# Moving the plain stores and loads of a fused convolution and dense-layer gradient kernel from SyncE's queue to GpSimd's

## The chip, the cores and the metric

The kernel runs on one core of a Trainium2 chip. The metric is the device time of one execution in microseconds (us), of which the median over several runs is given. A profile is one execution of the same program recorded by the hardware profiler.

The core has five instruction queues that matter here. PE is TensorE (matmuls; PEld its weight loads), DVE is VectorE, ACT is ScalarE, POOL is GpSimd, and SP is SyncE, which does no arithmetic and only issues DMAs (its rows in the timeline are called SPq). Each queue is worked off strictly in the order in which its instructions were written: an instruction that waits for a semaphore holds up all that stand behind it on the same queue.

## The reference, cut to what matters

The network has four layers over a sequence of 2048 rows of width 448: gated long convolution (A), dense layer with SiLU (B), A again with the same weights, B again with the same weights. The kernel returns the output and the gradients for q, k, v, shift_k, ssm_k, ssm_D, w1 and w2.

```
def A(q, k, v, shift_k, ssm_k, ssm_D):
    k_shift = 4-tap causal filter of k with shift_k
    kv = k_shift * v
    y = irfft(rfft(kv, 4096) * rfft(ssm_k, 4096))[:2048] + kv * ssm_D
    return q * y
def B(x, w1, w2):
    return silu(x @ w1) @ w2          # 448 -> 1792 -> 448
x = A_q
x = x + A(layernorm(x), k, v, ...)
x = x + B(layernorm(x), w1, w2)
x = x + A(layernorm(x), k, v, ...)
x = x + B(layernorm(x), w1, w2)
out = x;  gradients by jax.vjp with grad_out
```

The convolution result y doesn't depend on x, so it is computed once and used by both A layers.

## The kernel before, in words

**Three stages.** The head (class Head) computes the spectra of ssm_k and kv by a two-stage transform built of matmuls, multiplies them, and transforms back to y (tile Ysb). It ends at about 95 us. The main part (class Flow) walks over 16 tiles of 128 rows. The end (class Tail) forms the two weight gradients and the gradients of k, v and ssm_k.

**One tile of the main part** goes through: norm, gate, norm (n1); up through w1 (ps_h), SiLU and its slope on ACT (aT, dT); down through w2 (ps_o); norm, gate, norm (n3); up, SiLU and down again; then the backward pass: grad_out up through the transposed w2 (ps_g), times the slope (ghT), down through the transposed w1 (ps_n), the backward norm and gate, and the same once more for the first layer. Several tiles are in flight at a time. Each norm takes the power -0.5 of the variance on POOL (rstd, line 651); DVE needs it for the normalized tile n (line 652).

**Transposes.** An up step needs its input transposed (tile nT). For most tiles this is done by two DMA transposes that SP issues (lines 665 and 666 for n and G, lines 827 and 828 for grad_out). Ten of them at the two ends of the main part are done on PE.

**What is kept for the end.** The weight gradients need aT (both layers) and ghT (both layers) of all 16 tiles, so these are written to DRAM, 448 KB each, 64 stores in all. ghT is stored as it is in runs of 256 bytes (GH0 and GH1, `store`, line 740). aT is first transposed by a DMA transpose to the tile `turned` (line 746, ring of two buffers) and then stored in rows of 3584 bytes (A0 and A1, line 747). Both kinds are issued by SP. The normalized rows (N_d), the two outputs and the loads of grad_out and A_q rows go through POOL.

**The end.** `jobs("w2")` and `jobs("w1")` each walk over seven pairs p of 256 rows of the weight gradient. For each pair and each of two groups gi (the two layers) `bring` loads a 1 MB block jb from DRAM, and PE runs 2 x 16 matmuls of 448 columns over it (line 1200). jb is a ring of three buffers; two blocks of w1 use the buffer of Minv instead. For w2 the block is a plain load (line 1144; SP, only those of the first two pairs POOL). For w1 it is a DMA transpose out of GH0 or GH1 (line 1142, SP). The moving operand of w1 is the reloaded n (nmov, line 1124, SP). Results of w2 are stored through POOL (line 1226), those of w1 through SP (line 1228). Between the matmuls of these jobs PE does the inverse transforms for the gradients of k, v and ssm_k.

**What sets the order.** No instruction order is written by hand. Every step is an `s.op` with a cost per engine that could do it, a priority and, for DMAs, a kind and a number of bytes. `Sched.plan` runs these through a list scheduler: an engine that is free takes the ready step of lowest priority, a DMA's end is planned from its bytes, a rate per kind (RATE) and a constant (TAIL). `Sched.emit` then writes every engine's instructions in the planned order. The table NUDGE shifts single priorities, keyed by tile and kind of step. So a changed cost, rate or nudge changes the order of all five queues, and the order stays as planned however late a transfer is at run time.

Of the kernel before, what the change touches and what calls it, by code (L numbers as in the profile page):

```python
# [21 lines left out]
P = 128  # L22
S = 2048
D = 448
F = 1792
# [108 lines left out]
class Sched:  # L134
# [4 lines left out]
    STEP = 20  # L139
    TAIL = 1.5  # L140
    EPS = 1e-9
    RATE = {"plain": 410e3, "turn": 400e3, "load": 400e3, "rows": 280e3, "line": 280e3, "swap": 240e3}

# [239 lines left out]
class Head:  # L383
# [11 lines left out]
    def run(self, pr):  # L395
# [23 lines left out]
        for b in range(4):  # L419
            self.load(lambda b=b: ksb[b][:], k.A_ssm_k[128 * b:min(128 * b + 128, D), :], [ksb[b]], pr, 524e3 if b < 3 else 262e3)  # L420
        m1f = lambda: M1[:].rearrange("p a c k -> p (a c k)")
# [6 lines left out]
        k.w2 = s.vb("res", "W2", [P, NF * D], BF16, "w2sb")  # L428
        self.load(lambda: k.w2[:].rearrange("p (c d) -> p c d", d=D), k.B_w2.rearrange("(c p) d -> p c d", p=P), [k.w2], pr + 0.5, 1605e3)
        k.w2T = [s.vb("E", "w2T", [P, 3 * F], BF16, "w2T"), s.vb("PM", "w2Tr", [P, F], BF16, "w2T")]  # L430
        s.op({"SP": 9}, lambda e: nc.sync.dma_start_transpose(out=k.w2T[0][:].rearrange("p (c f) -> p c f", f=F), in_=k.B_w2[:, 0:384]), w=k.w2T[:1], prio=pr + 0.6, dma=("turn", 1376e3))
        for j in range(3):
# [96 lines left out]
        def conv(h, jq, q):  # L529
            pc = self.unit([P, 4, 256], name="ps_cv")  # L530

            def cv(e):
                for u in range(4):
                    j = 4 * jq + u
                    for c in range(2):
                        for t in range(4):
                            js = (j - t) % J
                            o = 1 if j >= t else 0
                            nc.tensor.matmul(pc[:, u, c * DC:(c + 1) * DC], lhsT=kT[h]()[:, js // 4, c, js % 4, o:o + 128], rhs=diag[h]()[:, c, t, :], start=(t == 0), stop=(t == 3))

# [5 lines left out]
            s.op({"POOL": 0.6}, lambda e: nc.gpsimd.dma_start(out=_pm(k.KS_d[:])[:, 4 * jq:4 * jq + 4, ds], in_=ks[:]), r=[ks], w=[ksv], prio=q + 20, dma=("plain", 230e3))  # L546
            s.op({"DVE": 0.54}, lambda e: nc.vector.tensor_tensor(out=kvt[:], in0=ks[:], in1=V.t[:, 4 * jq:4 * jq + 4, ds], op=ALU.mult), r=[ks, vs[jq // 2]], w=[kvt], prio=q)
            for u in range(0, 4, 2):
                n2 = 4 * jq + u
                ps = self.unit([P, 2, 2, 256], name="ps_s1")  # L550

                def s1(e, u=u, n2=n2, ps=ps):
                    for w in range(2):
                        for c in range(2):
                            nc.tensor.matmul(ps[:, w, c, :D // 2], lhsT=M1[:, n2 + w, c, :], rhs=kvt[:, u + w, :], start=True, stop=True)

                s.op({"PE": 0.4}, s1, r=[kvt, m1s[n2 // 8]], w=[ps], prio=q + 0, hold=[A1v])
                for w in range(2):
                    s.op({"ACT": 0.47, "DVE": 0.54}, lambda e, w=w, n2=n2, ps=ps: _copy(nc, e, A1v[:, 56 * h:56 * h + 56, :, n2 + w, :].rearrange("p dh c ds -> p c dh ds"), ps[:, w, :, :D // 2].rearrange("p c (dh ds) -> p c dh ds", ds=4)),
                         r=[ps], w=avs[7 * h:7 * h + 7], prio=q + 0)  # L560
# [56 lines left out]
EARLY = 2  # L617
ROWS = (0, 128, 256, 320)
TURNED = ((0, 1), (1, 1), (3, 0), (3, 1), (4, 0), (14, 1), (15, 0))
NUDGE = {(1, "ch"): 4, (4, "ch"): 0.4, (5, "ch"): 0.6, (6, "ch"): 4, (7, "ch"): 7, (13, "ch"): -0.2, (4, "cv"): -3, (6, "cv"): 4.2, (7, "cv"): 7, (1, "gG"): -8, (12, "gG"): 4, (14, "gG"): 6, (1, "h1"): 52, (2, "h1"): -3, (8, "h1"): -14, (4, "h2"): 11, (1, "kt"): -5, (2, "kt"): -9, (3, "kt"): -22, (5, "n1"): 4, (12, "n1"): 6, (10, "n2"): 3, (13, "n2"): 7, (14, "n2"): 7, (6, "o1"): -1, (10, "o1"): -2, (0, "s1"): -8, (2, "s1"): -9, (5, "s1"): -1, (6, "s1"): 5, (7, "s1"): -3, (9, "s1"): 1, (14, "s1"): 0.4, (15, "s1"): 2, (8, "s2"): 8, (10, "s2"): -2, (13, "s2"): 16, (3, "t1"): -11, (1, "t3"): -11, (15, "t3"): 6, (14, "tG"): -12, (0, "tg"): -44, (0, "tk"): 3, (1, "tk"): 2, (2, "tk"): 1, (6, "tk"): 20, (7, "tk"): 3, (8, "tk"): 4, (9, "tk"): 5, (10, "tk"): 3, (11, "tk"): 2, (12, "tk"): 11, (13, "tk"): 4, (3, "tt"): -0.2, (1, "tv"): -8, (2, "tv"): 5, (3, "tv"): 2, (8, "tv"): 16, (11, "tv"): -4, (13, "tv"): -12, (0, "w1"): 59, (5, "w1"): 14, (6, "x1"): -20, (7, "x1"): -20, (8, "x1"): -6, (8, "x3"): -7, (12, "xG"): 56, (0, "y"): 31}  # L620
NT1 = {1: "nTG", 2: "nT3", 3: "nT3"}
# [5 lines left out]
class Flow:  # L627
# [32 lines left out]
    def turn(self, src, pr, tag, on_pe, after=()):  # L660
        nc, k, s = self.nc, self.k, self.s
        if not on_pe:
            nT = self.small(tag, (P, ND, P))
            nT.name = "nT"
            s.op({"SP": 1.65}, lambda e: nc.sync.dma_start_transpose(out=nT[:, 0:3, :], in_=src[:, 0:384]), r=[src], w=[nT], prio=pr - EARLY, dma=("turn", 98e3))
            self.last_rows = s.op({"SP": 1.2}, lambda e: nc.sync.dma_start_transpose(out=nT[:, 3, :], in_=src[:, 320:448]), r=[src], w=[nT], prio=pr - EARLY, dma=("turn", 33e3))
            return nT
# [65 lines left out]
    def store(self, src, nm, j, pr):  # L733
        nc, s, k = self.nc, self.s, self.k
        dst = k.rows_d[nm]
        if nm not in RAW:
            self.store_turned(src, nm, j, pr)
            return
        at = dst.rearrange("(a p) s -> p a s", p=P)[:, :, P * j:P * j + P]
        s.op({"SP": 0.45}, lambda e: nc.sync.dma_start(out=at, in_=src[:]), r=[src], w=[k.st_[(nm, j)]], prio=pr, dma=("rows", 458e3))  # L740

    def store_turned(self, src, nm, j, pr):
        nc, s, k = self.nc, self.s, self.k
        dst = k.rows_d[nm]
        an = self.small("turned", (P, NF, P))
        s.op({"SP": 1.6}, lambda e: nc.sync.dma_start_transpose(out=an[:], in_=src[:].rearrange("p a s -> p (a s)")), r=[src], w=[an], prio=pr, dma=("turn", 458e3))
        s.op({"SP": 0.4}, lambda e: nc.sync.dma_start(out=dst[:, j, :], in_=an[:].rearrange("p a f -> p (a f)")), r=[an], w=[k.st_[(nm, j)]], prio=pr + 3, dma=("plain", 458e3))

# [41 lines left out]
    def tile(self, j):  # L790
# [35 lines left out]
        gT.name = "nT"  # L826
        s.op({"SP": 1.55}, lambda e: nc.sync.dma_start_transpose(out=gT[:, 0:3, :], in_=g[:, 0:384]), r=[g], w=[gT], prio=at("tg", c - 4), dma=("turn", 98e3))
        s.op({"SP": 1.2}, lambda e: nc.sync.dma_start_transpose(out=gT[:, 3, :], in_=g[:, 320:448]), r=[g], w=[gT], prio=at("tg", c - 4), dma=("turn", 33e3))
        gh2 = self.grad_up(gT, s2, at("g", c + 11.3), [up2] if j else [], not j)
# [38 lines left out]
class Tail:  # L868
# [242 lines left out]
    def jobs(self, which, pr):  # L1111
# [6 lines left out]
        else:  # L1118
            nm = [s.vb("PF", ("A1", "B1v")[i], [P, NT, D], BF16, "nmov") for i in range(2)]
            nh = [[v.sub() for _ in range(2)] for v in nm]  # L1120
            for i in (1, 0):
                for h in range(2):
                    hs = slice(8 * h, 8 * h + 8)
                    s.op({"SP": 0.4}, lambda e, i=i, hs=hs: nc.sync.dma_start(out=nm[i][:, hs, :], in_=_pm(k.N_d[i][:])[:, hs, :]),
                         r=[k.st_[("n", i, j)] for j in range(8 * h, 8 * h + 8)], w=[nh[i][h]], after=self.done[i], prio=pr - 30 if i else pr + 0.5, dma=("plain", 917e3), behind=k.loads[-1 - i:][:1])
# [34 lines left out]
        for p in range(NF // 2):  # L1160
# [66 lines left out]
            else:  # L1227
                s.op({"SP": 0.4}, lambda e, o=o, p=p: nc.sync.dma_start(out=out7[:, :, 256 * p:256 * p + 256], in_=o[:].rearrange("p c u f -> p c (u f)")), r=[o], prio=q, dma=("plain", 230e3))

# [75 lines left out]
def _rest(k):  # L1305
# [43 lines left out]
    k.w1T = s.vb("PM", "w1T", [P, NF * D], BF16, "w1T")  # L1349
    s.op({"SP": 2.0}, lambda e: nc.sync.dma_start_transpose(out=k.w2T[1][:], in_=k.B_w2[:, 320:448]), w=k.w2T[1:], prio=-100, dma=("turn", 460e3))  # L1350
    for h in range(2):
# [51 lines left out]
```

## Time and profile before

| | us |
|---|---|
| three runs | 718.8, 716.04, 714.32 |
| median | 716.04 |
| profiled execution, its own time | 722.49 |
| profiled execution, span from first to last instruction | 720.7 |
| PE busy | 686.6 |
| DVE busy | 518.2 |
| ACT busy | 408.1 |
| POOL busy | 161.1 |

Mean granted TensorE clock over the span: 0.99. The head is the first 95 us or so, the main part lasts to about 475 us, the end takes the rest. A busy time is the union of an engine's instructions; PE's is from modelled ends of pipelined matmuls. DMA share is the mean busy share of the 16 DMA engines; in single stretches it can read a little over 1. In the waits view a row reads: who waited, for what, how much in total, how many times, the longest. In the timeline a row reads: start, length, engine, line, operation, tiles, how many merged, and in brackets the idle time before it and who ended it. SP's rows are issue times: how long the queue was held by the instruction.

### The profile page before, as it was taken

The page shows a single profiled execution, that of the slowest core. Times are in us where ns is not written, and L with a number is a line of the kernel's source. Part 1 is how long each engine was busy: PE and PEld are TensorE (multiplying, and loading weights), DVE is VectorE, ACT ScalarE, POOL GpSimd, SP SyncE. Part 2 cuts the span into 40 slices and gives each one's busy share as a digit, 9 for nine tenths or more (in the row PEclk, how much of TensorE's full clock was granted, in tenths as well). Part 3 has the DMA queues.
Part 4 walks back from the last instruction along what each step waited for, and adds up shares of the span by engine and source line. Part 5 has one row for each costly group of instructions (what it writes and reads, how often), then busy time and mean ns, then how long its engine had stood idle before and what let it go on. Part 6 is the DMA issues. An engine that isn't in the chain of part 4 may idle for free. (4 is left out here: it accounts for less than half of the span.)

```text
span 720.7 us, 18096 instructions
## 1 busy us (share of the span) xinstructions
PE 686.6 (95%) x7496; PEld 476.6 (66%) x7512; DVE 518.2 (72%) x1206; ACT 408.1 (57%) x497; POOL 161.1 (22%) x274
## 2 busy tenths in 40 slices
PE   6999898999999899999999999999999999799997
PEld 4887666677676676776767776655777755345553
DVE  4979888768988868898888976764699758960000
ACT  4889887676667456766567664324877540014111
POOL 1233253203232122223222123022133131100000
PEclk9999999999999899999999999999999999899999
DMA  9959999967797777797786979956799669997961
GB/s 324 274 145 267 396 190 204 203 161 182 172 201 163 157 162 161 164 184 190 181 172 147 190 202 286 249 150 196 236 377 325 193 223 305 259 230 167 199 143 27
DMA packets 269727, 150.50 MB, mean 209 GB/s; under 512 B 224302, under 2 KB 250334, under 8 KB 269260
## 3 DMA queue, kind: packets, MB, share of 16 engines
q1 hardware_dynamic: 254494, 102.39, 62.0%
q0 software_dynamic: 14384, 46.14, 20.9%
q8 instruction: 59, 0.97, 0.6%
q10 hardware_dynamic: 766, 0.80, 0.4%
q14 instruction: 24, 0.20, 0.1%
HBM read 50.68 MB, written 54.60 MB: 146 GB/s over the span
## 5 line engine op out<-in xcount | busy, mean ns | idle before, releaser
L1200 PEld LDWEIGHTS <-jb 128*128 128x128 bf16 x892 | 85.8, 98 | 83.2 <-DMA jb<-GH_d 5.6
L1200 PE MATMUL ps_d<-nmov,jb 128*128 128x448 bf16 x448 | 90.0, 358 | 5.1 <-DMA jb<-GH_d 5.1
L692 PE MATMUL ps_h<-nT,w1sb 128*128 128x128 bf16 x1344 | 88.1, 222 | 5.7 <-DMA nT<-n 4.4
L755 PE MATMUL ps_n<-w1T,ghT 128*128 128x448 bf16 x448 | 90.0, 352 | 0.0
L755 PE MATMUL ps_o<-w2sb,aT 128*128 128x448 bf16 x448 | 89.5, 352 | 0.0
L692 PE MATMUL ps_g<-nT,w2T 128*128 128x128 bf16 x1344 | 86.1, 219 | 2.3 <-DMA nT<-G 2.3
L692 PEld LDWEIGHTS <-w1sb 128*128 128x128 bf16 x1344 | 78.6, 99 | 11.0 <-issue 4.0
L692 PEld LDWEIGHTS <-w2T 128*128 128x128 bf16 x1344 | 77.8, 98 | 10.8 <-issue 2.7
L93 ACT CAST ghp<-ps_g 128x896 bf16<-128x896 f32 x62 | 56.2, 907 | 42.9 <-PE ps_g L701 33.1
L729 ACT ACTIVATE aT<-ps_h 128x896 bf16<-128x896 f32 x64 | 56.8, 916 | 26.1 <-PE ps_h L701 17.6
L651 POOL TENSOR_TENSOR rstd<-ve,mhalf 128x1 f32<-128x1 f32 x64 | 41.0, 641 | 122.0 <-DVE ve L648 121.9
L755 PEld LDWEIGHTS <-ghT 128*128 128x128 bf16 x448 | 43.1, 98 | 37.8
L755 PEld LDWEIGHTS <-aT 128*128 128x128 bf16 x448 | 42.9, 98 | 36.7
L779 DVE SCALAR_TENSOR_TENSOR junk<-u,n 128x448 bf16<-128x448 bf16 x64 | 39.9, 623 | 31.7 <-ACT u L858 30.7
L729 ACT ACTIVATE dT<-ps_h 128x896 bf16<-128x896 f32 x60 | 53.2, 916 | 15.4 <-PE ps_h L701 10.5
L858 ACT ACTIVATE u<-ps_n,rstd 128x448 bf16<-128x448 f32 x32 | 20.3, 634 | 54.0 <-PE ps_n L755 24.6
L729 ACT ACT_TABLE_LOAD x38 | 48.8, 1283 | 0.7
L95 DVE COPY do<-ps_dt 112x512 bf16<-112x512 bf16 x2 | 0.8, 425 | 62.5 <-PE ps_dt L1221 62.5
L93 ACT CAST dob<-ps_d 128x448 bf16<-128x448 f32 x14 | 7.4, 532 | 67.6 <-PE ps_d L1200 67.6
L1200 PE MATMUL ps_d<-G,jb 128*128 128x448 bf16 x224 | 45.5, 352 | 0.2
L1200 PE MATMUL ps_d<-gmov,jb 128*128 128x448 bf16 x220 | 45.4, 353 | 0.1
L646 DVE BATCH_NORM_STATS2 st<-x 128x6 f32<-128x448 bf16 x64 | 40.0, 626 | 1.6
(180 smaller groups left out, 1270.0 us busy)
## 6 DMA issues: line engine op xcount, KB each, us to landing
A_d<-turned SPq DMA_DIRECT2D x32, 448.0 KB, 3.4
GH_d<-ghT SPq DMA_DIRECT2D x32, 448.0 KB, 4.7
jb<-A_d SPq DMA_DIRECT2D x10, 1024.0 KB, 6.8
KK<-KK POOLq DMA_DIRECT2D x14, 256.0 KB, 5.1
spec_KV<-X POOLq DMA_DIRECT2D x7, 512.0 KB, 9.5
spec_K<-KK POOLq DMA_DIRECT2D x7, 512.0 KB, 9.6
N_d<-n POOLq DMA_DIRECT2D x32, 112.0 KB, 4.2
sp_c<-spec_KV POOLq DMA_DIRECT2D x14, 256.0 KB, 6.7
```

What stands on the lines that cost most here:

```text
L93: nc.scalar.copy(out, in_)
L95: eng.tensor_copy(out, in_)
L646: nc.vector.bn_stats(out=st[:], in_=x[:])
L651: s.op({"POOL": 1.0}, lambda e: nc.gpsimd.tensor_tensor(out=rs[:], in0=ve[:], in1=self.k.mhalf[:, 0:1], op=ALU.pow), r=[ve], w=[rs], prio=pr)
L692: nc.tensor.matmul(ps[:, i, :], lhsT=at(b, ft), rhs=nT[:, b, :], **f)
L729: prev = [s.op({"ACT": 0.93}, lambda e, i=i, fun=fun, out=out, late=late: nc.scalar.activation(out[:, 7 * i:7 * i + 7, :], c[:, 7 * i:7 * ...
L755: nc.tensor.matmul(po[:, :D], lhsT=a[:, ft, :], rhs=wt[:, ft * D:(ft + 1) * D], start=(ft == 0), stop=(ft == NF - 1))
L779: nc.vector.scalar_tensor_tensor(out=junk[:], in0=u[:], scalar=1.0, in1=n[:], op0=ALU.mult, op1=ALU.mult, accum_out=cp[:, 1:2])
L858: s.op({"ACT": 0.85}, lambda e: nc.scalar.activation(u[:], pn[:, :D], ACT.Identity, scale=r[:], accum_out=cp[:, 0:1]), r=[pn, r], w=[u, cp ...
L1200: nc.tensor.matmul(ps[:, :D], lhsT=rows(t, gi, u), rhs=at(t), start=(first and t == ts[0]), stop=(last and t == ts[-1]))
```

## The change

Four things are changed.

1. The 64 stores of aT and ghT (lines 740 and 747) are issued by POOL instead of SP, and so are the four loads of nmov (line 1124) and the seven stores of the w1 gradient (line 1228). The condition `first` in `bring` also becomes true for p of 5 and 6, so four more plain blocks of jb go through POOL. In the main part SP then issues transposes only.
2. The planner's numbers: SP's cost of the transposes (1.25 us for each nT; 4.5 instead of 9 for w2T, 1.5 instead of 2 for its rest), a cost of 0.6 us for each store that POOL issues, TAIL 1.6 instead of 1.5, a new rate "short" for the stores of the shifted k, and larger byte counts for the loads of ssm_k and w2 in the head.
3. The table NUDGE is another one, 83 entries with other keys and values.
4. No step is added, no arithmetic is changed, and no buffer count is changed.

```
-    TAIL = 1.5
+    TAIL = 1.6
-    RATE = {"plain": 410e3, ..., "swap": 240e3}
+    RATE = {"plain": 410e3, ..., "swap": 240e3, "short": 140e3}
...
-            self.load(... k.A_ssm_k ..., [ksb[b]], pr, 524e3 if b < 3 else 262e3)
+            self.load(... k.A_ssm_k ..., [ksb[b]], pr, (1020e3, 524e3, 820e3, 750e3)[b])
...
-        self.load(... k.B_w2 ..., [k.w2], pr + 0.5, 1605e3)
+        self.load(... k.B_w2 ..., [k.w2], pr + 0.5, 2350e3)
-        s.op({"SP": 9}, ... dma_start_transpose(out=k.w2T[0] ...
+        s.op({"SP": 4.5}, ... dma_start_transpose(out=k.w2T[0] ...
...
-            s.op({"POOL": 0.6}, ... out=_pm(k.KS_d[:]) ..., dma=("plain", 230e3))
+            s.op({"POOL": 0.6}, ... out=_pm(k.KS_d[:]) ..., dma=("short", 230e3))
...
-NUDGE = {(1, "ch"): 4, (4, "ch"): 0.4, (5, "ch"): 0.6, ...
+NUDGE = {(0, "ch"): -2, (1, "ch"): 1, (2, "ch"): -6, ...
...
-            s.op({"SP": 1.65}, ... dma_start_transpose(out=nT[:, 0:3, :] ...
-            self.last_rows = s.op({"SP": 1.2}, ... dma_start_transpose(out=nT[:, 3, :] ...
+            s.op({"SP": 1.25}, ... dma_start_transpose(out=nT[:, 0:3, :] ...
+            self.last_rows = s.op({"SP": 1.25}, ... dma_start_transpose(out=nT[:, 3, :] ...
...
-        s.op({"SP": 0.45}, lambda e: nc.sync.dma_start(out=at, in_=src[:]), ..., dma=("rows", 458e3))
+        s.op({"POOL": 0.6}, lambda e: nc.gpsimd.dma_start(out=at, in_=src[:]), ..., dma=("rows", 458e3))
...
-        s.op({"SP": 0.4}, lambda e: nc.sync.dma_start(out=dst[:, j, :], in_=an[:]...), ..., prio=pr + 3, dma=("plain", 458e3))
+        s.op({"POOL": 0.6}, lambda e: nc.gpsimd.dma_start(out=dst[:, j, :], in_=an[:]...), ..., prio=pr + 3, dma=("plain", 458e3))
...
-        s.op({"SP": 1.55}, ... dma_start_transpose(out=gT[:, 0:3, :] ...
-        s.op({"SP": 1.2}, ... dma_start_transpose(out=gT[:, 3, :] ...
+        s.op({"SP": 1.25}, ... dma_start_transpose(out=gT[:, 0:3, :] ...
+        s.op({"SP": 1.25}, ... dma_start_transpose(out=gT[:, 3, :] ...
...
-                    s.op({"SP": 0.4}, lambda e, i=i, hs=hs: nc.sync.dma_start(out=nm[i][:, hs, :], ...
+                    s.op({"POOL": 0.6}, lambda e, i=i, hs=hs: nc.gpsimd.dma_start(out=nm[i][:, hs, :], ...
...
-            first = which == "w2" and p < 2
+            first = which == "w2" and (p < 2 or p > 4)
...
-                s.op({"SP": 0.4}, lambda e, o=o, p=p: nc.sync.dma_start(out=out7[:, :, 256 * p:256 * p + 256], ...
+                s.op({"POOL": 0.6}, lambda e, o=o, p=p: nc.gpsimd.dma_start(out=out7[:, :, 256 * p:256 * p + 256], ...
...
-    s.op({"SP": 2.0}, ... dma_start_transpose(out=k.w2T[1][:], in_=k.B_w2[:, 320:448]) ...
+    s.op({"SP": 1.5}, ... dma_start_transpose(out=k.w2T[1][:], in_=k.B_w2[:, 320:448]) ...
```

More of the change, by code (lines that the diff above doesn't have):

```diff
@@ L139 @@
     STEP = 20
-    TAIL = 1.5
+    TAIL = 1.6
     EPS = 1e-9
-    RATE = {"plain": 410e3, "turn": 400e3, "load": 400e3, "rows": 280e3, "line": 280e3, "swap": 240e3}
+    RATE = {"plain": 410e3, "turn": 400e3, "load": 400e3, "rows": 280e3, "line": 280e3, "swap": 240e3, "short": 140e3}
     def __init__(self, k, bufs, opener, start):
@@ L545, in conv @@
             s.op({"ACT": 0.8, "DVE": 1.0}, lambda e: _copy(nc, e, ks[:], pc[:, :, :D // 2]), r=[pc], w=[ks], prio=q)
-            s.op({"POOL": 0.6}, lambda e: nc.gpsimd.dma_start(out=_pm(k.KS_d[:])[:, 4 * jq:4 * jq + 4, ds], in_=ks[:]), r=[ks], w=[ksv], prio=q + 20, dma=("plain", 230e3))
+            s.op({"POOL": 0.6}, lambda e: nc.gpsimd.dma_start(out=_pm(k.KS_d[:])[:, 4 * jq:4 * jq + 4, ds], in_=ks[:]), r=[ks], w=[ksv], prio=q + 20, dma=("short", 230e3))
             s.op({"DVE": 0.54}, lambda e: nc.vector.tensor_tensor(out=kvt[:], in0=ks[:], in1=V.t[:, 4 * jq:4 * jq + 4, ds], op=ALU.mult), r=[ks, vs[jq // 2]], w=[kvt], prio=q)
@@ L739, in store @@
         at = dst.rearrange("(a p) s -> p a s", p=P)[:, :, P * j:P * j + P]
-        s.op({"SP": 0.45}, lambda e: nc.sync.dma_start(out=at, in_=src[:]), r=[src], w=[k.st_[(nm, j)]], prio=pr, dma=("rows", 458e3))
+        s.op({"POOL": 0.6}, lambda e: nc.gpsimd.dma_start(out=at, in_=src[:]), r=[src], w=[k.st_[(nm, j)]], prio=pr, dma=("rows", 458e3))
     def store_turned(self, src, nm, j, pr):
@@ L746, in store_turned @@
         s.op({"SP": 1.6}, lambda e: nc.sync.dma_start_transpose(out=an[:], in_=src[:].rearrange("p a s -> p (a s)")), r=[src], w=[an], prio=pr, dma=("turn", 458e3))
[L747 removed]
+        s.op({"POOL": 0.6}, lambda e: nc.gpsimd.dma_start(out=dst[:, j, :], in_=an[:].rearrange("p a f -> p (a f)")), r=[an], w=[k.st_[(nm, j)]], prio=pr + 3, dma=("plain", 458e3))
     def down(self, a, wt, name, pr):
@@ L1123, in jobs @@
                     hs = slice(8 * h, 8 * h + 8)
-                    s.op({"SP": 0.4}, lambda e, i=i, hs=hs: nc.sync.dma_start(out=nm[i][:, hs, :], in_=_pm(k.N_d[i][:])[:, hs, :]),
+                    s.op({"POOL": 0.6}, lambda e, i=i, hs=hs: nc.gpsimd.dma_start(out=nm[i][:, hs, :], in_=_pm(k.N_d[i][:])[:, hs, :]),
                          r=[k.st_[("n", i, j)] for j in range(8 * h, 8 * h + 8)], w=[nh[i][h]], after=self.done[i], prio=pr - 30 if i else pr + 0.5, dma=("plain", 917e3), behind=k.loads[-1 - i:][:1])
@@ L1227, in jobs @@
             else:
-                s.op({"SP": 0.4}, lambda e, o=o, p=p: nc.sync.dma_start(out=out7[:, :, 256 * p:256 * p + 256], in_=o[:].rearrange("p c u f -> p c (u f)")), r=[o], prio=q, dma=("plain", 230e3))
+                s.op({"POOL": 0.6}, lambda e, o=o, p=p: nc.gpsimd.dma_start(out=out7[:, :, 256 * p:256 * p + 256], in_=o[:].rearrange("p c u f -> p c (u f)")), r=[o], prio=q, dma=("plain", 230e3))
 @with_exitstack
```

18 lines of the change are left out of this document (9 added, 9 removed).

## The prediction

> **What bounds the kernel now.** I read the page's table of busy time first, then the same table in stretches, then who waits for whom, then the timeline of the two places where PE waits longest.
>
> ```profile
> PE 686.6 (95%) x7496; PEld 476.6 (66%) x7512; DVE 518.2 (72%) x1206; ACT 408.1 (57%) x497; POOL 161.1 (22%) x274
> PE   6999898999999899999999999999999999799997
> ```
>
> PE is the bound. 720.7 − 686.6 = 34.1 us of the span is PE idle, and no reordering can win more. By stretches it is 14.7 us up to 120 us, 0.9 from 120 to 160, 5.9 from 160 to 520 and 12.7 behind that. In the steady main part the up steps through w1 that belong to the same layer start at 357.1, 379.5 and 401.9 us: 22.4 us a tile, with PE busy throughout.
>
> ```profile
> PE ps_kt L456 <- DMA K_sb<-in_A_ssm_k_dram: 5.3, 2, 4.7
> PE ps_d L1200 <- DMA jb<-GH_d: 5.1, 1, 5.1
> PE ps_h L692 <- DMA nT<-n: 4.4, 3, 2.4
> PE ps_g L692 <- DMA nT<-G: 2.3, 2, 1.4
> ```
>
> These are PE's four largest waits, and all are for a DMA. The first is the start of the program. The other three are for transposes that SP issues, so I look at SP just before them.
>
> ```profile
> 234.86 2.85 SPq L746 DMA_TRANSPOSE turned<-aT  x1
> 237.76 1.25 SPq L828 DMA_TRANSPOSE nT<-g  x1
> 242.81 0.33 SPq L747 DMA_DIRECT2D A_d<-turned  x1
> 243.24 1.21 SPq L665 DMA_TRANSPOSE nT<-n  x1
> ...
> 245.94 0.38 PE L692 MATMUL ps_h<-nT,w1sb 128*128 128x128 bf16 x2 [2.42 <-DMA nT<-n]
> 247.32 1.97 PE L692 MATMUL ps_h<-nT,w1sb 128*128 128x128 bf16 x17 [1.00 <-DMA nT<-n]
> ```
>
> SP stands still from 239.0 to 242.8: the store of `turned` waits until its transpose has landed, and the nT that PE needs is queued behind that store. PE loses 2.4 + 1.0 us. Over the whole main part this kind of wait is
>
> ```profile
> SPq L747 <- DMA turned<-aT: 18.1, 13, 5.3
> ```
>
> SP has little room to absorb it: its rows from 200 to 400 us add up to 178 us of issuing. The second place is in the end:
>
> ```profile
> 594.70 0.52 SPq L1144 DMA_DIRECT2D jb<-A_d  x1
> 595.40 13.05 SPq L1142 DMA_TRANSPOSE jb<-GH_d  x1
> 608.54 1.00 SPq L1124 DMA_DIRECT2D nmov<-N_d  x2
> 609.63 29.49 SPq L1142 DMA_TRANSPOSE jb<-GH_d  x4
> ...
> 626.68 3.17 PE L1200 MATMUL ps_d<-nmov,jb 128*128 128x448 bf16 x8 [5.13 <-DMA jb<-GH_d]
> ```
>
> The first transposed block stands behind the last plain block, holds SP for 13 us, two reloads of n follow, and only then is the second block issued, which lands 17.0 us later and lets PE wait 5.13 us.
>
> **The change, part by part.**
>
> *Main part, stores off SP.* In the 200 us just named, the 17 + 17 stores held SP for 20 us, and the waits of line 747 come on top. Both leave SP's path to nT. PE's waits for nT there are 3.4 us (243 us), 0.94 (320), 1.41 (436) and 0.88 (144). The first is caused by a store, so I take all of it; at 320 the second nT transpose held SP for 3.66 us behind crowded neighbours, I take it too; of the one at 144, half. The one at 436 I leave: from 428.89 on, POOL issued three 1 MB blocks and the nT issued beside them took 8 us to land, which doesn't change. Gain 3.4 + 0.9 + 0.4 = 4.7 us; bounds 0 and the whole 6.6.
>
> *End, blocks of p = 5 and 6 and nmov off SP.* The first transposed block needs Minv's buffer, free when the last inverse transform ends at 586.6; SP could issue it near 590 instead of 595.4. The second needs a buffer that PE gives back at about 601.4. With 1.0 us of nmov gone from between and the first one earlier, it can be issued at about 603; with the 17.0 us of before it lands at 620, before PE asks at 621.55. Gain 5.1 us; bounds 0 (if the DMA engines set this, below) and 5.1.
>
> *Given back.* TensorE's granted clock was halved in two stretches, and PE's waits lay partly in them:
>
> ```profile
> 246.00:253.00 7.00, 6.00 (x62) 5.45 (x63) 4.77 (x16) 1.16 (x2) 0.54 (x1) 0.51 0.94 158
> 625.00:632.00 7.00, 5.32 (x45) 2.37 (x46) 6.97 (x11) 0.00 (x0) 1.08 (x2) 0.52 1.22 266
> ```
>
> Idle PE in them is 1.0 and 1.7 us. If PE works there instead and the stretches stay, half of that work is not gained: +1.3 us; bounds 0 and 1.3.
>
> *POOL's own time.* What a POOL issue costs grows with the number of runs:
>
> ```profile
> L546 POOL DMA_DIRECT2D KS_d<-ks x8: 752/792/802, 28.2 to 52.5; - x8
> L1144 POOL DMA_DIRECT2D jb<-A_d x4: 1208/1222/1237, 428.9 to 474.9; - x4
> L1226 POOL DMA_DIRECT2D out_dram<-do x7: 707/720/757, 482.0 to 615.7; - x7
> ```
>
> The first has 512 runs, the second 2048. A store of ghT has 1792 runs: on the straight line between them 0.79 + 1280 / 1536 × 0.43 = 1.15 us (estimate). So 32 × 1.15 + 32 × 0.54 (as the 128-run N_d) + 4 × 1.22 + 4 × 0.55 + 7 × 0.72 = 66 us more on an engine that is busy 161 of 720. In the main part it goes from about 6 to 9.4 us of each 22.4 us tile, so POOL doesn't become a bound by work.
>
> *POOL's waits.* Queued behind a waiting store on POOL are the rstd of the norms (64 of 0.64 us), and for rstd waits DVE (line 652, today 8.4 us in 14 times), behind it all else on DVE, then nT and PE. Cover: DVE is idle 4.5 us of each 40 in the steady part. Bounds: nothing, if the new order leaves each rstd enough room; 18.1 us, if every wait of line 747 reaches PE. Nearest row: today's waits for rstd, which cost PE nothing. I take +1.5, near the low end, for about one store in twenty getting through with its 1.15 us.
>
> *Later landings.* A 224 KB result lands 7.3 us (median) after POOL's issue and 2.8 after SP's; 4.5 us later holds buffers longer. A ghT lives from its up step (198.6) to the landing of its store (211.4), 12.8 us, and its ring of four turns once in 22.4 us: 9.5 us are spare, so this costs 0; without that cover, up to the 4.5 us.
>
> *Last stores.* The last one is issued at 716.94 and lands 2.79 later; nothing hides it. POOL issues in 0.72 instead of 0.32; its landing is between 2.3 (quickest 224 KB row of POOL) and 10.2 us (slowest, in DMA traffic). The DMA share at the end is 0.09, so I take 3.3: +0.9 us; bounds −0.1 and +7.8.
>
> *Head and order.* No instruction is added or removed; the new costs and nudges permute the same work. PE's idle time from 20 to 120 us is 8.2 us, mostly behind ACT and DVE copies. I can't tell which order comes out: 0, bounds −4 and +4, half of it either way.
>
> Sum: −4.7 − 5.1 + 1.3 + 1.5 + 0.9 + 0 = −6.1 us. The profiled execution took 722.49 us, 1.8 around its span; it would take 716.4. The median of the runs is 716.04, less 6.1 makes 709.9; I say 710.
>
> **Rivals.**
>
> *The DMA engines set the end, and SP still waits.* From 600 to 620 us the DMA share reads 1.16, and the same bytes have to move. If bandwidth and not SP's queue made the second block late, the 5.1 us stay, and of the half clock only 0.5 comes back: −4.7 + 0.5 + 1.5 + 0.9 = −1.8, time 714.2. For it: the share; SP's `turned` transposes still wait for ACT (22.1 us for ghp alone). Against it: in the quieter stretch behind 650 us a block holds SP 4.3 us, a third of 13. The Trainium skill says the same (DMA: Bandwidth & Descriptors, "Issuing engines are not separate DMA queues"): all issuers share 16 engines, and spreading saves only sequencer time; by that alone the end would gain nothing. The trace agrees as far as that share goes, but also shows SP standing still, which the rule doesn't count.
>
> *The wait moves to POOL (slower).* Place: a store of `turned` on POOL, planned for a landing that comes late, ahead of an rstd. It decides from the point where the delay is longer than DVE's and nT's room. Price up to the 18.1 us of line 747, in place of my 1.5: −6.1 − 1.5 + 18.1 = +10.5, time 726.5. For it: turned lands 5.5 us after issue in the median but up to 10.7, and the order is fixed beforehand. Against it: only 3.4 us of those 18.1 reached PE on SP, where nT stood directly behind. The Trainium skill adds a cause (SBUF — State Buffer, "Who interferes with whom"): VectorE in its two-port modes locks GpSimd out while it writes descriptors. No row here shows it: N_d is issued in 0.54 to 0.59 us beside a VectorE busy 89%.
>
> *More closes than I count.* The new order also removes 436 (1.4), the rest of 144 (0.5), a wait of 1.4 at 577 and the 4 us of the head: −6.1 − 7.3 = −13.4, time 702.6. For it: the whole table of nudges is new; against it: nothing in the trace says that the head gets better.
>
> **How the numbers follow.** Chances: forecast 0.38 (own range 703 to 716), bandwidth 0.18, wait on POOL 0.28 (716 to 730, spread by how much of 18.1 arrives), more 0.16. Taking 1% (7.2 us) as what a measurement can tell from no change: faster than 708.9 is 0.42 of the forecast, nearly all of "more" and a little of bandwidth, 0.32; above 723.2 is three quarters of the POOL case and a little of the others, 0.24; between, 0.44. The range that leaves two in ten out is 700 to 728.
>
> **What would show it right or wrong.** Right: no wait of PE for jb<-GH_d over 1 us; the second transposed block issued before 605; nT waits of PE under 3 us in all behind 120 us; POOL near 225 us busy; GH_d stores on POOL at 1.0 to 1.3 us each. Wrong: DVE's waits for rstd well over 8.4 us, POOL waiting for turned with PE idle behind it, or a longer head.

## The result, and the profile after

The changed kernel takes 755.75 us (median of 4 runs, 753.97 to 769.04), the kernel before beside it 715.56 (714.32 to 718.80): ratio 1.055, 95% interval 1.050 to 1.060. Executions that ran slow, here the one of 769.04 us, are left out of every ratio. The forecast was 710, its range 700 to 728. The profiled execution took 753.97 us, its span 751.1.

The table of busy time and the timeline in 40 slices (PE, granted clock, DMA share) of the changed kernel's page:

```profile
PE 687.0 (91%) x7495; PEld 474.4 (63%) x7512; DVE 518.3 (69%) x1205; ACT 408.9 (54%) x498; POOL 226.9 (30%) x353
PE   6999889999999998999999999999999706799996
PEclk9999999999999999999999999999999956989998
DMA  9959999797877787787877789979978999999960
```

Its waits, those of PE for a DMA:

```profile
PE ps_d L1200 <- DMA jb<-A_d: 30.6, 2, 28.8
...
PE ps_d L1200 <- DMA jb<-GH_d: 2.6, 1, 2.6
PE ps_h L692 <- DMA nT<-n: 1.5, 3, 0.9
PE ps_g L692 <- DMA nT<-G: 1.0, 1, 1.0
```

PE works as long as before (687.0 against 686.6 us). The slices show one hole, a 0 at 600 us, and half the clock in it. One wait of 28.8 us makes it. Split at 570 us, PE's idle time is 20.0 us before that point (22.0 in the kernel before) and 44.1 behind it (12.0): −2.0 + 32.1 + 0.4 of PE's own time is, but for rounding, the 30.4 us by which the span grew. The main part is not where the time went; the end is.

The timeline of that place, SP, POOL and PE (start, length, engine, line, tiles; in brackets the idle time before):

```profile
573.79 1.18 POOL L1144 DMA_DIRECT2D jb<-A_d  x1
576.47 31.14 SPq L1142 DMA_TRANSPOSE jb<-GH_d  x1
583.19 1.21 POOL L1144 DMA_DIRECT2D jb<-A_d  x1 [2.21 <-PE ps_d L1200]
584.40 0.55 POOL L1124 DMA_DIRECT2D nmov<-N_d  x1
585.67 0.56 POOL L1124 DMA_DIRECT2D nmov<-N_d  x1
...
605.51 1.17 POOL L1144 DMA_DIRECT2D jb<-A_d  x1
606.67 0.55 POOL L1124 DMA_DIRECT2D nmov<-N_d  x1
625.15 1.30 PE L1200 MATMUL ps_d<-gmov,jb 128*128 128x448 bf16 x3 [28.82 <-DMA jb<-A_d]
```

SP issues the first transposed block 2.7 us behind a plain 1 MB block of POOL. The transpose holds SP for 31.14 us and lands 51.8 us after its issue; the next one, issued at 607.73, holds SP for 38.3. The plain block that POOL issued at 583.19 lands 41.9 us later, and it is the one PE waits for. The reloads of n land 38.2 us after their issue in the median, 9.9 in the kernel before. All of them are late together, on both queues. The windows of 10 us say how (columns: window, length, busy time of PE, PEld, DVE, ACT, POOL, granted clock, DMA share, GB/s):

```profile
590.00:600.00 10.00, 6.33 (x62) 3.11 (x60) 0.00 (x0) 1.06 (x2) 0.00 (x0) 1.00 1.13 213
600.00:610.00 10.00, 0.00 (x0) 0.00 (x0) 8.48 (x11) 0.00 (x0) 2.25 (x3) 0.51 1.28 133
610.00:620.00 10.00, 0.00 (x0) 0.00 (x0) 5.76 (x15) 0.00 (x0) 0.55 (x1) 0.50 1.37 46
620.00:630.00 10.00, 4.85 (x43) 2.15 (x44) 0.00 (x0) 0.00 (x0) 1.17 (x2) 0.50 0.91 227
```

The DMA engines read as fully busy and move 46 GB/s; the kernel before moved 278 in the same ten microseconds:

```profile
610.00:620.00 10.00, 10.00 (x112) 5.25 (x110) 9.89 (x16) 1.06 (x2) 1.81 (x3) 1.00 1.11 278
```

The packet records of 610 to 620 us say the same: the transposes' 256-byte packets took 229 ns in the median, where such packets took 18 ns with no plain load beside them (kernel before, 650 to 660 us). This is not a full pipe but a collapsed one.

### The profile page after: what moved, and what is told of

It reads as the page before. It is cut to its first block, busy times and chain, and to the rows that moved or that the text cites. A ratio compares the mean times of both kernels' runs of the same rounds, so it can differ in the third digit from the quotient of the medians.

```text
span 751.1 us, 18109 instructions
## 1 busy us (share of the span) xinstructions
PE 687.0 (91%) x7495; PEld 474.4 (63%) x7512; DVE 518.3 (69%) x1205; ACT 408.9 (54%) x498; POOL 226.9 (30%) x353
## 5 line engine op out<-in xcount | busy, mean ns | idle before, releaser
L692 PE MATMUL ps_h<-nT,w1sb 128*128 128x128 bf16 x1344 | 85.6, 219 | 4.9 <-DVE nT L95 2.6
L1200 PE MATMUL ps_d<-gmov,jb 128*128 128x448 bf16 x220 | 47.7, 365 | 28.9 <-DMA jb<-A_d 28.8
L93 ACT CAST do<-ps_d 128x448 bf16<-128x448 f32 x13 | 6.9, 532 | 71.7 <-PE ps_d L1200 71.7
L747 POOL DMA_DIRECT2D A_d<-turned x32 | 17.9, 561 | 87.2 <-DMA turned<-aT 86.6
```

What stands on the lines that cost most here:

```text
L93: nc.scalar.copy(out, in_)
L692: nc.tensor.matmul(ps[:, i, :], lhsT=at(b, ft), rhs=nT[:, b, :], **f)
L747: s.op({"POOL": 0.6}, lambda e: nc.gpsimd.dma_start(out=dst[:, j, :], in_=an[:].rearrange("p a f -> p (a f)")), r=[an], w=[k.st_[(nm, j)]] ...
L1200: nc.tensor.matmul(ps[:, :D], lhsT=rows(t, gi, u), rhs=at(t), start=(first and t == ts[0]), stop=(last and t == ts[-1]))
```

## The experiments

**Theories.** A: DMA transposes on SP's queue and large plain loads on POOL's queue, in flight together, slow each other far below what either does alone. B: POOL's queue delivers these loads late by itself. C: the DMA engines are simply full there. D: the queues are harmless, and the new order asks for too much at once.

**One part undone: blocks, reloads, both.** e1 gives the blocks of p = 5 and 6 and nmov back to SP, e2 the blocks alone, e3 nmov alone.

```
e1, e2:  -  first = which == "w2" and (p < 2 or p > 4)
         +  first = which == "w2" and p < 2
e1, e3:  -  nc.gpsimd.dma_start(out=nm[i][:, hs, :], ...
         +  nc.sync.dma_start(out=nm[i][:, hs, :], ...
```

> The changed kernel with two of its moves undone: the blocks of p = 5 and 6 of the w2 job and the four reloads of nmov are issued by SyncE again, so that they stand in one queue with the transposed blocks; everything else, main part and head included, stays as changed. Theory A (two queues at once: transposed 1 MB blocks from SyncE's queue and plain 1 MB transfers from GpSimd's queue, in flight together, hold each other up): PE's wait of 28.8 us goes, no plain block takes over 15 us to land, and the time is 716 to 723 (755.8 less 28.8 + 1.8 + 2.6 + 3.9 = 37 of waits, plus up to 5 for the old wait for the second transposed block). Theory B (GpSimd's transfers are slow for a reason of their own: descriptors, VectorE): the moved blocks are quick again, but the eight 224 KB stores of gkp and the stores of ksf that stay with GpSimd still take over 15 us, time 735 to 750. Theory C (the DMA engines are simply full between 576 and 660 us): same bytes, same delay, 745 to 757.

> The changed kernel with only the blocks of p = 5 and 6 of the w2 job back on SyncE; nmov (4 x 896 KB) stays on GpSimd. Theory A: the long wait of PE for jb<-A_d goes, since these blocks now stand in front of the transposed blocks in the same queue; nmov on GpSimd's queue still meets the first transposed block, so a shorter wait for nmov or for jb<-GH_d is left, 5 to 20 us; time 720 to 742. Theory B: jb quick, nmov still slow by itself: 725 to 745 with nmov landing over 25 us even where no transpose is in flight. Theory C: 745 to 757.

> The changed kernel with only nmov back on SyncE; the blocks of p = 5 and 6 stay on GpSimd. Theory A: the first transposed block is still issued before the last plain blocks, and these still wait in the other queue: PE waits 10 to 30 us for jb<-A_d, time 730 to 757, depending on whether nmov now stands ahead of the transposes. Theory B: the same time as changed less the share of nmov, 740 to 755. Theory C: 745 to 757.

Measured: e1 1.0035 (0.9991 to 1.0079), median 721.57; e2 1.0028 (0.9985 to 1.0071), 718.70; e3 1.032 (1.024 to 1.040), 737.37. Taking four 1 MB blocks off POOL's queue gives back some 37 us (the difference of the ratios times 715.6), more than theory A expected of e2; taking nmov off gives back 16. In e3 PE's largest wait is still for a block of POOL:

```profile
PE ps_d L1200 <- DMA jb<-A_d: 20.3, 2, 15.0
```

So the loss hangs on which plain loads POOL has in flight beside the transposes, the blocks more than nmov.

**The overlap by itself.** m1 runs DMAs alone, in phases.

> No part of the reference is computed and most outputs are left unwritten; it measures transfers by themselves, in ten stretches with a barrier between them. A warm-up, then: three 1 MB transposed blocks on SyncE alone; four plain loads (two of 917 KB in runs of 512 bytes, two of 1.8 MB in runs of 14 KB) on GpSimd alone; the same loads on GpSimd beside the same transposes on SyncE; loads and then transposes all on SyncE; loads on ScalarE's queue beside the transposes on SyncE; eight 224 KB stores on GpSimd beside the transposes; the same stores on ScalarE's queue beside the transposes; eight pairs of small transposes from on-chip memory alone, with four 448 KB stores in runs of 256 bytes on GpSimd, and with these stores on SyncE. Theory A: beside GpSimd's loads the stretch takes more than twice the sum of both alone (over 60 us against about 13 + 15), and the one on SyncE alone takes about the sum. Whether ScalarE's queue does the same tells if it is GpSimd or any second queue. Theory B: GpSimd's loads alone already take over 30 us. Theory C: every mixed stretch takes the sum of its parts, 25 to 30 us, whichever queue.

Measured, first issue to last landing: three 1 MB transposes on SP 15.7 us; two short (512-byte runs) and two long (14 KB runs) plain loads on POOL 18.3; both at once 51.2, with loads landing up to 40 us after their issue instead of up to 16 (theory A expected over 60). All seven behind each other on SP's queue took 31.3, the loads on ACT's queue beside the transposes 35.6, stores on POOL beside them 19.4. Loads on POOL alone are quick, so B falls; and the same bytes on one queue take 31.3 us, so C falls: full engines would give at most the sum, 34.0. A stands. Two more phases bear on the main part: eight pairs of small transposes like those of nT took 21.6 us alone, 27.8 beside four 448 KB stores on POOL, and 27.4 with these stores in SP's own queue. There the move of the stores gained nothing.

**The end's moves alone, in the order of before.**

```
 (kernel before)
-  nc.sync.dma_start(out=nm[i][:, hs, :], ...
+  nc.gpsimd.dma_start(out=nm[i][:, hs, :], ...
-  first = which == "w2" and p < 2
+  first = which == "w2" and (p < 2 or p > 4)
```

> The kernel before with one part of the change alone: the blocks of p = 5 and 6 of the w2 job and the four reloads of nmov go through GpSimd; main part, head, planner numbers and nudges stay as before. Theory A (transposed 1 MB blocks on SyncE's queue and plain 1 MB loads on GpSimd's queue starve each other): the first transposed block is issued before the last plain ones have landed, plain blocks take over 20 us to land, PE waits 15 to 40 us, ratio to before 1.02 to 1.06. Rival D (the new costs and nudges of the change make the end slow, whichever queue the loads use): ratio 0.99 to 1.01.

Measured: 709.68 us (709.47 to 710.80), ratio 0.990 (0.987 to 0.992): faster than both kernels, and against what theory A expected. The same transposes and the same loads share the same two queues:

```profile
580.79 5.03 SPq L1142 DMA_TRANSPOSE jb<-GH_d  x1
...
582.58 1.18 POOL L1144 DMA_DIRECT2D jb<-A_d  x1 [1.88 <-PE ps_d L1200]
...
585.61 0.56 POOL L1124 DMA_DIRECT2D nmov<-N_d  x1
...
586.67 0.55 POOL L1124 DMA_DIRECT2D nmov<-N_d  x1
...
595.48 15.21 SPq L1142 DMA_TRANSPOSE jb<-GH_d  x1
```

Here no plain block of POOL is in flight when the first transposed block is issued (the one before, issued at 558.91, had landed 8.7 us later); the next follows 1.8 us behind it. The transpose holds SP for 5.0 us instead of 31.1, nmov lands after 13.2 us (median), the second transpose starts at 595.5 and PE never waits for it: the 5.1 us of the kernel before are gone. This second transpose did meet loads in flight, a plain block issued at 589.02 that landed at 603.19 and all four parts of nmov, and yet landed after 17.2 us. A needs an addition: the overlap can collapse, but it need not.

**The overlap prevented, everything on its new queue.** In e5 SP writes a few bytes out of the last two plain blocks and the four parts of nmov before the first transposed block; SP's queue therefore stands until they have landed. e10 does it for the two blocks only.

```
+  def landed(e):
+      for x, (b, _) in enumerate(k.plain):
+          nc.sync.dma_start(out=k.seen[x:x + 1, :], in_=b[0:1, 0, 0:64])
+      ...                            # e5 alone: the same for the four parts of nmov
+  k.load = [s.op({"SP": 2.5}, landed, r=[...], prio=pr - 30, ...)]
```

> The changed kernel with all its queues; only a small addition on SyncE ahead of the first transposed block: six stores of 128 bytes that read the last two plain blocks and the four parts of nmov, so that no transposed block is issued before these have landed. Theory A: the plain loads land in under 15 us, PE's wait for jb<-A_d of 28.8 us goes; as the first transposed block now starts late, PE waits 5 to 15 us for it instead: time 725 to 745, ratio 1.015 to 1.04. Rival C (the DMA engines are full): the loads stay slow and the transposes come later still, over 755. Rival B (GpSimd's loads slow by themselves): over 755.

> The changed kernel with two 128-byte stores on SyncE that read the last two plain blocks, ahead of the first transposed block, so that this is issued only when these two have landed; nmov stays free to overlap (with the guard over nmov too the ratio was 1.004). Theory 'the first transposed block met GpSimd's 1 MB blocks too early': no collapse, first transposed block near 590 to 600, ratio 0.985 to 1.01. Theory 'transposed blocks collapse beside nmov alike': landings of 30 us and more, ratio over 1.02.

Measured: e5 1.0044 (1.0014 to 1.0074), 720.99 us; e10 1.0054 (1.0013 to 1.0094), 719.50. Both take back some 35 us although SP stands idle for them. In e5 nmov lands after 10.3 us in the median and PE's waits are small (its line 1210 is line 1200 of the changed kernel):

```profile
PE ps_d L1210 <- DMA jb<-GH_d: 4.9, 3, 2.8
```

With no load moved off POOL's queue and no collapse, B and C fall in the kernel itself too. e10 can't say whether nmov alone would collapse a transpose: its first transposed block went out at 606.25 us, and the last part of nmov landed 4.4 us later.

**All loads of the end on SP.**

```
-  first = which == "w2" and (p < 2 or p > 4)        +  first = False
-  nc.gpsimd.dma_start(out=nm[i]...                  +  nc.sync.dma_start(out=nm[i]...
```

> The changed kernel with all plain loads of jb and nmov on SyncE, those of the first two pairs as well, which were on GpSimd before and after; stores stay on GpSimd. Theory A: no large load is left on GpSimd's queue beside transposes but gmov and the constants; the waits for jb<-A_d at the start of the end (12.8 us in one execution of the kernel with the end's loads back on SyncE) go too and the executions scatter less; time 706 to 716, ratio 0.985 to 1.0. Rival D: the new order itself holds the rest, ratio 1.0 to 1.01, scatter as before.

Measured: 1.0008 (0.9977 to 1.0038), 719.38 us, where rival D had it and not theory A. In e1, e2 and e6, which keep the new order, the interval holds 1: what that order and the other moves win is not told apart from nothing.

The wait of 12.8 us that theory A meant to remove is, in e1's trace, for gmov and not for a block jb, and gmov stays on POOL in e6. That one execution (734.32 us) shows a second collapse: the transpose of `turned` issued at 448.08 held SP for 19.55 us and landed after 35.9, and three of the four 448 KB loads of gmov beside it landed after 28.9 to 30.3 us. In e6's profiled execution three of them took 22.6 to 24.6 us and PE waited 6.7; in the changed kernel's the slowest took 12.4.

**What in the overlap does it?** m2 takes the kinds apart, m3 repeats the mix, e9 cuts nmov into short runs inside the changed kernel.

> No part of the reference is computed and the outputs are left unwritten; it measures transfers by themselves in stretches with a barrier between them: after a warm-up, two 1.8 MB loads in 14 KB runs on GpSimd; two 917 KB loads in 512-byte runs on GpSimd; three transposed blocks alone; the long-run loads on GpSimd beside the transposes; the short-run loads on GpSimd beside the transposes; the long-run loads ahead of the transposes on SyncE; the long-run loads on ScalarE's queue beside the transposes; eight 112 KB loads on GpSimd beside the transposes; six transposes of 448 KB from on-chip memory alone; these beside the long-run loads on GpSimd; beside the short-run loads on GpSimd; the small transposes beside the short-run loads on GpSimd; one long-run load on GpSimd beside one transposed block. Theory A in the form 'bytes loaded on GpSimd's queue beside transposes': both kinds of run lose, in proportion to their bytes (long-run 15 to 20 us over the sum of both alone, short-run 5 to 10), and transposes from on-chip memory lose as well. Rival A2 (only the short runs, whose descriptors are many): long runs cost no more than the sum. Rival A3 (only transposes that read DRAM): those from on-chip memory cost no more than the sum.

Measured in m2: two long loads beside the three transposes 25.2 us, two short ones 29.4, against sums of 28.4 and 26.5: the one is under its sum, the other 2.9 over it, and neither is a collapse, so bytes alone do not do it. But six 448 KB transposes from on-chip memory (14.9 alone) beside two long loads (11.4) took 41.3, and beside two short ones 21.3: a transpose need not read DRAM for it.

> Nothing of the reference is computed: phases of DMAs only, with all engines brought together in between. A phase has up to three 1 MB DMA transposes from DRAM on SyncE's queue and up to four plain loads on GpSimd's: short ones (917 KB in 512-byte runs), long ones (1.8 MB in 14 KB runs), or the mix short, long, short, long. Earlier the mix beside the transposes took 51 us in the one time it was tried (sum of the two alone 34), two short or two long ones beside them 25 to 29 (no loss). Phases: warm-up; transposes alone; mix alone; mix with transposes three times over; the same with GpSimd some 4 us late; with SyncE some 4 us late; four short ones with the transposes; four long ones with them; mix with a single transpose; four short ones alone. Theory 'the amount in flight decides': the mix collapses in all three repeats (over 45 us each), four short and four long ones do so too, whatever the offset. Theory 'it takes both run lengths': the mix collapses, four of one kind stay at or under the sum of their parts. Theory 'order and moment decide': the three equal repeats differ, or the two offsets differ, by over 8 us.

Measured in m3: mix alone 18.2 us, transposes alone 15.5, so 33.7 in all. Three equal phases of both took 46.5, 29.2 and 49.3. The windows of the first two, from POOL's first issue to about its last landing (length, busy DVE and POOL, clock, DMA share, GB/s):

```profile
98.00:137.00 39.00, 0.16 (x1) 3.27 (x4) 1.00 1.09 180
147.00:169.00 22.00, 0.16 (x1) 3.28 (x4) 1.00 1.01 320
```

The same instructions move at 320 GB/s once and at 180 the other time, with the DMA share over 1 in both. In the issue times the one difference is that POOL started 0.73 us behind SP in the quick phase and 0.42 and 0.41 in the slow ones. With POOL made late by two tiny loads it took about 40, with SP late 51, and the mix with a single transpose 32, where the two alone add up to 24.7. So order and moment matter. Four short loads took 32, four long ones 34 (to the end of the last issue), which suggested that both run lengths are needed.

```
-  nc.gpsimd.dma_start(out=nm[i][:, hs, :], in_=_pm(k.N_d[i][:])[:, hs, :])
+  [nc.gpsimd.dma_start(out=nm[i][:, hs, c], in_=_pm(k.N_d[i][:])[:, hs, c]) for c in (slice(0, 256), slice(256, D))]
```

> The changed kernel with each of the four loads of nmov cut into two DMAs with runs of 512 and 384 bytes instead of 7168 (same bytes, same queue, same place; GpSimd issues four instructions more). All plain loads beside the transposed blocks are then of short runs. Theory 'it takes short and long runs together beside the transposes' (equal phases with the mix took 46.5, 29.2 and 49.3 us, four loads of one kind 32 and 34): no transposed block and no plain load lands later than 25 us, the wait of 28.8 us is at most 10, ratio 0.99 to 1.025. Theory 'any 1 MB loads on GpSimd's queue beside a transposed block do it': landings of 35 us and more, ratio 1.04 or more.

Measured: 759.38 us, ratio 1.054 (1.040 to 1.068), no better than the changed kernel. The issue of its first transposed block in the timeline, PE's two largest waits, and the DMA view of nmov (size and median us to landing), now all in short runs:

```profile
577.46 28.67 SPq L1142 DMA_TRANSPOSE jb<-GH_d  x1
```

```profile
PE ps_d L1200 <- DMA jb<-A_d: 24.3, 2, 19.3
PE ps_d L1200 <- DMA jb<-GH_d: 16.2, 2, 10.3
```

```profile
nmov<-N_d POOLq DMA_DIRECT2D x4, 512.0 KB, 33.7
nmov<-N_d POOLq DMA_DIRECT2D x4, 384.0 KB, 33.6
```

The idea of the run lengths falls. The moment at which the streams meet is left, which these runs support but do not vary by itself in the kernel.

**The other part alone, and all moves in the order of before.** e7 is the kernel before with only lines 740 and 747 on POOL; e8 adds e4's moves and the last seven stores. Nudges and planner numbers stay those of before.

```
e7, e8:  -  s.op({"SP": 0.45}, lambda e: nc.sync.dma_start(out=at, in_=src[:]), ...
         +  s.op({"POOL": 0.6}, lambda e: nc.gpsimd.dma_start(out=at, in_=src[:]), ...
         -  s.op({"SP": 0.4}, lambda e: nc.sync.dma_start(out=dst[:, j, :], in_=an[:]...
         +  s.op({"POOL": 0.6}, lambda e: nc.gpsimd.dma_start(out=dst[:, j, :], in_=an[:]...
```

> The kernel before with one part of the change alone: the 64 stores of aT and ghT (lines 740 and 747) on GpSimd instead of SyncE, at a planned 0.6 us each; nudges and all other planner numbers stay, the end is as before. The prediction's steps for this part: 4.7 us gained from nT, 1.5 given to waits on GpSimd: -3 us, ratio 0.993 to 0.998 counting the given-back clock. The theory that the main part gains nothing, since nT waits shrink and waits for rstd grow alike: 0.998 to 1.006. The theory that the waits of line 747 now reach TensorE through rstd: over 1.01.

> All queue moves of the change (64 stores, four plain blocks, nmov, the last seven stores), but the nudges and the planner's other numbers of before. If the loss lies in the moment at which the first transposed block meets GpSimd's loads, and the order of before keeps them apart as it did with the end's moves alone (0.990): 0.985 to 1.0, first transposed block landing within 20 us. If the stores of the main part on GpSimd's queue bring the overlap about, whatever the order: 1.03 or more, with transposed blocks landing in 35 us and more and the share of the DMA engines over 1 at under 150 GB/s.

Measured: e7 1.017 (1.013 to 1.021), 729.90 us, as the third theory expected; e8 1.011 (1.008 to 1.015), 724.04, between its two forecasts. e8's first transposed block holds SP for 5.0 us and lands after 10.7: the stores of the main part don't bring the collapse about. Theory D falls as it was put, since e1, e2, e5 and e6 keep the new order and come out at most 0.5% slower: the large loss takes the overlap and the new order together. What the stores do is seen in e7's waits:

```profile
PE ps_n L755 <- DVE ghT L768: 14.3, 6, 4.9
...
POOL A_d L747 <- DMA turned<-aT: 107.1, 29, 12.8
...
DVE n L652 <- POOL rstd L651: 42.8, 26, 6.2
```

The longest of them, step by step in the timeline:

```profile
207.01 4.58 SPq L746 DMA_TRANSPOSE turned<-aT  x1
...
218.20 0.58 POOL L747 DMA_DIRECT2D A_d<-turned  x1 [6.64 <-DMA turned<-aT]
218.80 0.57 POOL L651 TENSOR_TENSOR rstd<-ve,mhalf 128x1 f32<-128x1 f32 x1
...
219.40 0.40 DVE L652 TENSOR_SCALAR n<-x,mv,rstd 128x448 bf16<-128x448 bf16 x1 [6.25 <-POOL rstd L651]
...
221.55 1.68 PE L755 MATMUL ps_n<-w1T,ghT 128*128 128x448 bf16 x4 [4.85 <-DVE ghT L768]
```

The transpose lands 10.6 us after its issue, POOL stands 6.6 us in front of the store, the rstd behind it is late, then DVE, then PE.

## Why the prediction was wrong, point by point

**The step that failed** is "End, blocks of p = 5 and 6 and nmov off SP": "with the 17.0 us of before it lands at 620 ... Gain 5.1 us; bounds 0 ... and 5.1". It took the landing time that a transposed block had behind loads on its own queue and used it for one with loads beside it on another queue, and its bounds left no room for a loss. In the changed kernel the second block was issued at 607.73, not by 603, and landed 46.1 us later. The term came out at +32, outside its bounds. That the overlap is the cause is shown by removal (e1, e2, e5, e10) and by itself (m1, m3). The nearest row had been in front of me: an nT landed after 8 us beside POOL's 1 MB blocks issued from 429 us on, against a median of 2.6 for its line 666. I read that as a fixed price and not as a sign of what the two streams do to each other.

**The mechanism of that term was right all the same.** In the order of before (e4) the moves bring what was promised: the second block issued at 595.5, no wait of 5.1 us, the whole kernel 1.0% faster. The 5.1 us had been read from an execution 6.4 us above the kernel's median, so the profiled spans differ by 13.0 us (720.7 and 707.7) and the medians by 7.2. What turned a gain into a loss is the new order with its planner numbers. It puts a plain block of POOL 2.7 us ahead of the first transposed block, where e4 and e8 have it 1.8 us behind.

**The rival from the DMA engines** (714.2) read their share of 1.16 as a limit of bytes. The rule quoted there from the Trainium skill (DMA: Bandwidth & Descriptors, "Issuing engines are not separate DMA queues"), that spreading over queues saves only sequencer time, would by itself have made the move worth nothing. Neither covers what happened, a share of 1.37 at 46 GB/s. And e4, 1.0% faster, shows that moving loads to another queue can pay.

**The wait that moves to POOL** had its place and mechanism right, and its price nearly: e7's chain above is that rival link by link. For e7's part alone the rival's sum is −4.7 + 18.1 = +13.4 us, and e7 lost 1.7% (12 us). In the changed kernel the new order absorbs it: POOL waits 86.6 us for `turned` (SP waited 18.1), DVE 22.7 for rstd instead of 8.4, but from 120 to 480 us PE idles 4.8 us, before 6.7, in e7 15.7. nT gave 4.2 us back and other waits, 2.0 of them for DVE's line 834, took some 2.3 of it again; that these come from POOL is not shown. So the +1.5 was near for this order and far too low for the other. The new order and planner numbers earn in the main part what the queue moves cost there, and lose it in the end.

**nT.** PE's waits for nT fell from 6.7 to 2.5 us, against a forecast of 4.7 gained: right in the mechanism, 0.5 us short.

**"Given back", +1.3, had the wrong sign.** The term let the slow stretches stay. But the half clock follows PE's longer waits rather than standing at a fixed place. In the changed kernel it begins at 600.2, 3.9 us after PE stopped, and lasts until 630.9, 5.8 us after PE resumed. In e4 both stretches of the kernel before, around 246 and 625 us, are at full clock. PE's busy time there is 679.9 us, before 686.6. A closed wait takes its slow stretch with it: an estimated 3.4 us each (half of 6.8 us at half clock, and half of that difference).

**Held:** POOL's busy time (226.9 us, near 225 expected), a ghT store on POOL (1.12 us on average against 1.15), the head (PE idle 14.5 us up to 120 us, before 14.7), DVE not shutting POOL out of its issuing (GH_d issues stay at 1.1 us, and in the hole DVE was idle from 590 to 600). The last store lands 2.92 us after its issue, so its term was +0.1 rather than +0.9; a landing is counted from the start of the issue, so 0.4 of the 0.9 had been counted twice.

**Still open:** why one overlap collapses and its twin does not. Not the run lengths (e9), not the bytes in flight (e4 and e8 have the same), not POOL's stores (m1's and m3's mix has none). Nor is it enough that a transpose meets a plain load already in flight: that fits the first block in the changed kernel, e3 and e9, but e4's second block met such loads without a collapse, and in m3 SP was first in all three equal phases, of which two collapsed.

The packet records show one thing that goes with it. A 1 MB transpose is 4096 packets of 256 bytes. In e4, e8 and m3's quick phase 4009, 4032 and 4006 of the first block's packets had started before the first packet of the loads issued behind it; in the changed kernel 601, and in the phases with the mix that took 46 to 51 us (m1, m3) 2254 to 3052. It isn't the whole rule: the phase with POOL late had 4025 and still took 40 us, and two long loads in m2 came after 1036 and did not collapse. No run varies this alone.

## What to carry to other kernels

When a load moves to another queue, it no longer stands in line behind its neighbours but runs beside them: price the pair and not the issue time, above all where one of the two is a DMA transpose. Where large plain loads on one queue and large DMA transposes on another overlap, look at how long both take to land; if they collapse, keep them apart in time, if need be by putting the transpose behind the landing of the load. The wait this costs (1.004 for the whole kernel) is small against a collapse (1.055). And try the queue moves one by one in the old order: here one of them alone was worth 1.0%, and the package with its new order lost 5.5%.

## What the runs showed of the hardware that was not expected

- DMA transposes on SP's queue beside 1 MB plain loads on POOL's queue can fall to 46 GB/s together, at a DMA share of 1.37, with landings of 26 to 52 us instead of 6 to 17 in the kernel before; 256-byte packets then took 229 ns instead of 18.
- The same phase took 29.2 us once and 46.5 and 49.3 us the other times (m3). Behind each other on one queue the same bytes took 31.3 us, in the one phase that ran so (m1).
- Transposes from on-chip memory do it too: 41.3 us beside two long loads in the one phase of m2, where the two took 14.9 and 11.4 alone.
- Stores on POOL's queue beside transposes cost little: eight of 224 KB beside three 1 MB transposes took 19.4 us, the transposes alone 15.7 (m1). Four of 448 KB beside eight pairs of small transposes cost more, 27.8 against 21.6, and as much on SP's queue (27.4).
- PE's granted clock halved 3.3 to 4.9 us into a long wait and came back 2.7 to 5.8 us after work resumed: idle from 621.6 to 626.7 us and half from 624.9 to 631.7 before, 596.3 to 625.2 and 600.2 to 630.9 in the changed kernel, 597.3 to 616.6 and 602.2 to 619.3 in e9.
